# Down products of the last four inner blocks of a ReLU² MLP: float16 in three parts instead of fp32r in two

## Chip, cores and metric

The kernel runs on one core of a Trainium2 chip. The metric is the device time of one execution in microseconds (us). TensorE is called PE in the profile, its weight loads PEld, VectorE DVE, ScalarE ACT, GpSimd POOL, and SyncE, which issues most DMAs, SP.

## What is computed

Attention with a relative bias for 4 batches of 8 heads, 576 positions and head size 64; its result, as a matrix `x` of 2304 rows and 512 columns, goes through a two-layer MLP:

```
x = attn_out.transpose(0, 2, 1, 3).reshape(B * S, H * D)   # 2304 x 512
h = x @ w_in                                               # 512 x 2048
r = np.maximum(h, 0.0)
g = r * r
out = g @ w_out                                            # 2048 x 512
```

The inputs and the output are fp32. The products must come out at fp32's accuracy, so each factor is split into a high part and what is left over, and a product is a sum of three partial products.

## The kernel before

The first 320 us or so are attention, the rest is the MLP, and the change touches the MLP. The rows of `x` are taken in five blocks: n = 0 to 3 are 512 rows of each batch, and n = 4 (called `B` in the code) are the 4 times 64 rows left over. The 2048 inner columns are taken in eight inner blocks P = 0 to 7 (`NP` is 8). A pair (n, P) is an item; there are 40 of them, in the order that `runs` gives (L1171): items 0 to 11 are blocks 0, 1 and 2 with P = 0 to 3, items 12 to 17 block 3 with P = 0 to 5, items 18 to 31 blocks 0 to 3 with the rest of their P up to 7, and items 32 to 39 are block `B` with P = 0 to 7. So the inner blocks 4 to 7 are items 16 to 31, of full width (w = 256), and items 36 to 39, of half width (w = 128).

The loop at L1317 runs once for each item, and its iteration i works on item i and on the item before it:

- `products(i)` (L1198) makes the up products in a seven-product scheme (Strassen's): 42 float16 matmuls of w columns, 24 into the PSUM tile `ha` and 18 into `hb`.
- `parts_g(i-1)` (L1240) splits the squared activations `c` of the item before: ACT copies them to fp32r (`gh`), DVE subtracts (`gl`).
- `lead` and `high_out` or `sums_in`, `high_in`, `low_in` prepare one 128-row piece of a weight for later use: n = 4P+2 and 4P+3 are the pieces of `w_out` of inner block P. `lead_at` (L1179) says in which iteration. `high_out` (L727) makes an fp32r copy on ACT and the rest on POOL.
- `sums(i)` (L1214) puts the seven products together on ACT (one pass) and DVE (four) and scales them by `alpha`; `squares(i)` applies ReLU and the square, on ACT up to item 31, on DVE after that (`GA`, L1234).
- `down(i-1)` (L1287) makes the down products: 24 matmuls of 512 columns (12 for block `B`) into four (two) PSUM tiles `y`, a third with each of (gh, wh), (gh, wl), (gl, wh). At the end of a run `leave` (L1260) takes `y` out and stores it.

On PE the order is therefore `products(0)`, `products(1)`, `down(0)`, `products(2)`, `down(1)` and so on, written out by hand: under `manual_schedule` each engine works in program order, SP's queue too. Where iteration i-1 has looked for the largest entry of a block of x (`largest_at`: i-1 = 4, 8, 28), a one-column fp32 matmul with a matrix of ones (L1328) stands between `products(i)` and `down(i-1)`; it spreads a column's sum over all partitions, and five small DVE instructions after `sums(i)` (`scale_of`, L772, with `power_of`, L219) make a scale of it. Raw pieces of `w_out` come by DMA (`fetch_out`, L697); the last eight (18, 19, 22, 23, 26, 27, 30, 31) one per iteration from iteration 4 on (L1353).

Of the kernel before, what the change touches and what calls it, by code (L numbers as in the profile page):

```python
# [70 lines left out]
XC = 8  # L71
MAGIC = 8388608.0

HI_MIN, HI_MAX = (float(x) for x in np.array([0x38000000, 0x47EFFFFF], np.uint32).view(np.float32))
# [3 lines left out]
def attention_then_relu2_mlp(ctx: ExitStack, tc: tile.TileContext, q, k, v, cols, w_in, w_out, psi, xmat, dist, out):  # L78
# [101 lines left out]
    ins = [n for n in range(2 * NF) if n // 2 % 2 == 0]  # L180
    small = keep.tile([128, 72], F32, name="small")
    used = [0]

    def column(w=1):
        used[0] += w
        return small[:, used[0] - w:used[0]]

# [30 lines left out]

    def power_of(ps_col):  # L219
# [3 lines left out]
        DVE.tensor_scalar(out=ti, in0=ti, scalar1=0x7F800000, scalar2=None, op0=ALU.bitwise_and)  # L223
        DVE.tensor_scalar(out=si, in0=ti, scalar1=-1.0, scalar2=266 * 2.0 ** 23, op0=ALU.mult, op1=ALU.add)
        DVE.tensor_scalar(out=isig, in0=top, scalar1=2.0 ** -12, scalar2=None, op0=ALU.mult)
        return sig, isig
# [5 lines left out]

    def top_w():
        m = column()
        mi = m.bitcast(I32)
        largest(wcols, m)
        DVE.tensor_scalar(out=m, in0=m, scalar1=HI_MIN, scalar2=HI_MAX, op0=ALU.max, op1=ALU.min)
        t = column()
# [488 lines left out]
    def high_out(n):  # L727
        copy_out(n)
        rest_out(n)

# [34 lines left out]
    ORDER = (2, 3, 4, 5, 1, 6, 7)  # L765
    xs_t = {}

    def set_scale(n, cols, ps_col):
# [3 lines left out]
    def scale_of(n, ps_col):  # L772
        xsig[n], isig = power_of(ps_col)
        alpha_t[n] = column()
        DVE.tensor_tensor(out=alpha_t[n], in0=wscale[1], in1=isig, op=ALU.mult)
# [233 lines left out]
    def scan(k):  # L1009
        scan_w(k)  # L1010
        if k + len(raws) < NF:
            fetch_in(ins[k + len(raws)], raws[(k - SCANS) % len(raws)])
        if k == NF - 1:
            jobs.insert(len(norms), [now[0] + 1, [("DVE", 0.75, lambda: power_job(now[0] + 1, top_w(), scaled))]])
# [164 lines left out]
    lead_at = {1: (6, 7), 2: (10, 11), 3: (14,), 4: (15,)}  # L1179
    lead_at.update({5: (16,), 9: (17,), 12: (20,), 13: (21,), 14: (18, 19), 15: (22, 23)})  # L1180
    lead_at.update(zip(range(18, 26), ((n,) for n in range(24, 32))))
# [3 lines left out]
    largest_at = {4: 2, 8: 3, 28: B}  # L1185
    raw_outs = [18, 19, 22, 23, 26, 27, 30, 31]
    raw_ins = [n for n in ins if n not in early]
# [7 lines left out]
    c_t, g_t, y_t = {}, {}, {}  # L1195
    scales = []

# [16 lines left out]
    def sums(i, ha, hb):  # L1214
        n, P = items[i]
        w = width[n]
        alpha = alpha_t[n]
        if i % 2:
            c, s = (take(1, o, 1024).rearrange("p (m t) -> p m t", m=4)[:, :, :w] for o in (4480, 5504))
        elif i < NP // 2:  # L1220
            c, s = (tmp_p.tile([128, 4, 256], F32, name=x, tag=x) for x in "cs")
        else:
            c, s = (xT[1][:, :, 256 * x:256 * x + w] for x in range(2))
        ACT.activation(out=s, in_=ha[:, :, :w], func=AF.Identity, scale=alpha)
        stt = DVE.scalar_tensor_tensor
        stt(out=c[:, 2:4], in0=ha[:, 1:3, :w], scalar=alpha, in1=s[:, 0:4:3], op0=ALU.mult, op1=ALU.subtract)
        stt(out=c[:, 0:2], in0=ha[:, 2:4, :w], scalar=alpha, in1=s[:, 0:2], op0=ALU.mult, op1=ALU.add)  # L1227
        stt(out=c[:, 2:4], in0=hb[:, 0:1, :w].to_broadcast([128, 2, w]), scalar=alpha, in1=c[:, 2:4], op0=ALU.mult, op1=ALU.add)
        stt(out=c[:, 2:4], in0=hb[:, 1:3, :w], scalar=alpha, in1=c[:, 2:4], op0=ALU.mult, op1=ALU.add)
        c_t[i] = c  # L1230

    def squares(i):
# [4 lines left out]
        else:  # L1237
            DVE.scalar_tensor_tensor(out=c, in0=c, scalar=0.0, in1=c, op0=ALU.max, op1=ALU.mult)

    def parts_g(i):  # L1240
        c, w = c_t[i], width[items[i][0]]
        for f in range(2):
            gl = mlp.tile([128, 2, 256], F32R, name="gl", tag="gl", bufs=2)[:, :, :w]
            gh = mlp.tile([128, 2, 256], F32R, name="gh", tag="gh", bufs=2)[:, :, :w]
# [42 lines left out]
    def down(i):  # L1287
# [25 lines left out]
    with tc.manual_schedule():  # L1313
        for n in (6, 7, 10, 11, 14, 15):
            fetch_out(n)
        fetch_in(raw_ins.pop(0))
        for i in range(NI + 1):  # L1317
            if i == NP // 2:
# [106 lines left out]
```

## Time and profile before

| | us |
|---|---|
| median of 3 runs | 697.07 (697.04 to 697.47) |
| the profiled execution: its own time | 697.57 |
| its span, from the first to the last instruction | 695.8 |
| PE busy, share of the span | 97% |
| granted clock of PE, mean over the span | 0.997 |

The profiled execution's time is 1.8 us more than its span and 0.5 us above the median. The profile's views used below are the page (busy time by engine), the windows (busy time of each engine in a stretch), the chain of waits (the work that ended last, followed back), the timeline (instructions in order of time, merged where they repeat) and the groups of instructions by line and shape. A matmul's duration in these views is longer than the step from its start to the next one's start, since matmuls overlap in the pipeline; where the text needs the step it divides the time from one group's start to the next one's by the count.

### The profile page before, as it was taken

What the parts mean: (1) busy time and instruction counts of PE and PEld (TensorE: products, weight loads), DVE (VectorE), ACT (ScalarE), POOL (GpSimd) and SP (SyncE); (2) the same over time, 40 slices, a digit from 0 to 9 for tenths busy, and PEclk for the clock granted to TensorE, in tenths of its full rate; (3) what the DMA queues carried; (4) which work ended last, traced back from release to release, by engine and by line L of the source; (5) the groups of instructions that cost most, each with busy time, mean ns of one, the idle gap of its engine ahead of it and who ended that gap; (6) DMA issues with size and microseconds to landing.
All of it is one profiled execution on the core that took longest, in us unless ns stands there. A gap on an engine that the chain in (4) does not pass through costs nothing.

```text
span 695.8 us, 17950 instructions
## 1 busy us (share of the span) xinstructions
PE 676.8 (97%) x7238; PEld 561.5 (81%) x7238; DVE 549.9 (79%) x1165; ACT 473.2 (68%) x960; POOL 196.5 (28%) x313
## 2 busy tenths in 40 slices
PE   6899999999999999999999999999999999999997
PEld 5578888887877878778788888888888888888886
DVE  8999989877788898998888969777477775567664
ACT  5678888888777989997666756766466664447221
POOL 6465545442112343653223205112020112001000
PEclk9999999999999999999999999999999999999999
DMA  6740000017476134111901443050057222633101
GB/s 188 205 128 13 20 2 3 2 63 206 152 266 196 55 116 131 47 33 57 367 2 62 152 167 122 14 214 1 1 194 291 106 77 106 227 121 122 62 1 31
DMA packets 31682, 75.16 MB, mean 108 GB/s; under 512 B 5616, under 2 KB 13936, under 8 KB 30576
## 3 DMA queue, kind: packets, MB, share of 16 engines
q1 hardware_dynamic: 31440, 73.76, 31.1%
q8 instruction: 57, 0.93, 0.6%
q14 instruction: 25, 0.20, 0.1%
q10 hardware_dynamic: 160, 0.26, 0.1%
HBM read 55.66 MB, written 18.35 MB: 106 GB/s over the span
## 4 chain that ended last, share of the span: by engine, by line
PE 86%; DVE 8%; ACT 2%; issue 2%; POOL 1%; DMA 0%; ACTq 0%; POOLq 0%; DVEq 0%
PE y L1302 29%; PE ha L1210 13%; PE sp L425 11%; PE px L565 10%; PE hb L1210 10%; PE bb L383 5%; PE pp L529 3%; PE pp L534 3%; DVE t L438 2%; DVE mask L373 1%; PE pa L547 1%; ACT pt L1141 1%; DVE bt L391 1%; ACT p L445 1%; DVE xT L496 0%
## 5 line engine op out<-in xcount | busy, mean ns | idle before, releaser
L1210 PEld LDWEIGHTS <-area 128*128 128x128 f16 x1680 | 147.7, 98 | 25.3 <-issue 8.4
L1302 PE MATMUL y<-w,gh 128*128 128x512 f32 x576 | 149.0, 398 | 0.6 <-ACT gh L1246 0.6
L1302 PEld LDWEIGHTS y<-w,gh 128*128 128x128 f32 x576 | 105.1, 188 | 22.2 <-ACT gh L1246 1.3
L438 DVE CUSTOM_DVE_ANT_0 t<-sp,area 128x576 f32<-128x576 f32 x144 | 104.2, 753 | 21.2 <-PE sp L425 10.3
L445 ACT ACTIVATE p<-t,negm 128x576 f32<-128x576 f32 x144 | 112.9, 794 | 2.7 <-DVE negm L438 2.1
L425 PE MATMUL sp<-k,q 64*128 64x288 f32 (+1 forms) x640 | 99.4, 428 | 5.5 <-DVE negm L438 3.9
L565 PE MATMUL px<-pt,v 128*64 128x128 f32 (+1 forms) x1600 | 92.2, 266 | 0.0
L565 PEld LDWEIGHTS px<-pt,v 128*64 128x64 f32 x1600 | 79.2, 137 | 10.7 <-ACT pt L1141 6.0
L1210 PE MATMUL ha<-area 128*128 128x256 f16 (+1 forms) x816 | 85.1, 260 | 0.7 <-DVE c L1227 0.7
L399 POOL TENSOR_TENSOR area<-bt,bt 128x256 f32<-128x256 f32 x72 | 65.9, 922 | 64.1 <-DVE bt L391 63.9
L1302 PE MATMUL y<-w,gl 128*128 128x512 f32 x288 | 79.0, 390 | 0.0
L425 PEld LDWEIGHTS sp<-k,q 64*128 64x128 f32 (+1 forms) x640 | 53.3, 176 | 25.5 <-issue 6.0
L1210 PE MATMUL hb<-area 128*128 128x256 f16 (+1 forms) x612 | 64.7, 260 | 0.0
L1302 PEld LDWEIGHTS y<-w,gl 128*128 128x128 f32 x288 | 54.1, 188 | 12.2 <-DVE gl L1247 0.2
L373 DVE TENSOR_TENSOR mask<-sdist,theta 128x1024 f16<-128x1024 f16 x81 | 57.3, 711 | 1.0 <-PE bb L383 0.8
L869 ACT COPY pt<-pp 128x512 f32<-128x512 f32 (+1 forms) x76 | 37.4, 544 | 24.9 <-PE pp L534 24.7
L383 PEld LDWEIGHTS <-mask 128*128 128x128 f16 x1296 | 45.9, 99 | 9.5 <-DVE mask L373 6.4
L383 PE MATMUL bb<-wmov,mask 128*128 128x64 f16 x1296 | 47.5, 193 | 5.5 <-DVE mask L373 4.7
L1141 ACT COPY pt<-pp 128x512 f32<-128x512 f32 x76 | 41.4, 601 | 12.8 <-PE pp L529 12.3
L1247 DVE TENSOR_TENSOR gl<-area,gh 128x512 fp32r<-128x512 f32 (+1 forms) x40 | 25.3, 668 | 27.3 <-ACT gh L1246 25.5
L738 POOL TENSOR_TENSOR raw<-wa 128x256 f32<-128x256 f32 x16 | 12.2, 761 | 120.9 <-issue 66.1
L388 ACT ACTIVATE bt<-bb,small 128x256 f32<-128x256 f32 x81 | 39.1, 486 | 7.1 <-PE bb L383 5.2
(164 smaller groups left out, 1062.2 us busy)
## 6 DMA issues: line engine op xcount, KB each, us to landing
raw<-in_w_in SPq DMA_DIRECT2D x32, 512.0 KB, 4.4
r<-in_w_out SPq DMA_DIRECT2D x16, 512.0 KB, 5.4
xs<-area SPq DMA_DIRECT2D x4, 1792.0 KB, 11.1
py<-o SPq DMA_DIRECT2D x12, 512.0 KB, 4.1
o<-py SPq DMA_DIRECT2D x12, 512.0 KB, 4.1
v<-in_v SPq DMA_DIRECT2D x16, 320.0 KB, 4.0
q<-in_q SPq DMA_DIRECT2D x32, 128.0 KB, 3.0
out<-o SPq DMA_DIRECT2D x8, 512.0 KB, 2.9
```

What stands on the lines that cost most here:

```text
L373: DVE.tensor_tensor(out=out, in0=win, in1=th, op=ALU.is_ge)
L383: PE.matmul(bb[:, 64 * (7 - r):64 * (8 - r)], lhsT=m[:, r], rhs=wmov[:, n], start=(n == 0), stop=(n == 1))
L388: ACT.activation(out=sv, in_=bv[:, 1], func=AF.Identity, scale=bscale)
L399: POOL.tensor_tensor(out=dst, in0=tw, in1=sw, op=ALU.add)
L425: mm = PE.matmul(out_t[to, x, :HALF], lhsT=qt[rows, cols], rhs=kt[rows, k0:k0 + HALF], start=True, stop=True)
L438: DVE.tensor_tensor_reduce(out=t.rearrange("p (x n) -> p x n", x=2), in0=sp[:, :, :HALF], in1=bias.rearrange("p (x n) -> p x n", x=2), sca ...
L445: ACT.activation(out=p[:, S * n:S * n + S], in_=t, func=AF.Exp, bias=negm[:, n:n + 1], scale=-1.0, accum_out=sums[:, 2 * ic + n:2 * ic + n ...
L565: PE.matmul(px[64 * h:64 * h + 64, 128 * m:128 * m + w], lhsT=vt[:, c, h], rhs=src, start=(c == 0), stop=(c == 4))
L869: ACT.copy(dst, src)
L1141: ACT.copy(*c)
L1210: PE.matmul(h[:, s, :w], lhsT=a, rhs=x, start=(k == 0), stop=(k == 5))
L1302: PE.matmul(y_t[n][k], lhsT=(gl if m == 2 else gh)[:, slot, o:o + 128], rhs=wl if m == 1 else wh, start=((n, P) in firsts and f == 0 and m ...
```

## The change

All partial products of the inner blocks 4 to 7 become float16 by float16. A float16 has as many significant bits as are wanted of a high or low part but little range, so scales (powers of two) are worked out at run time. `w_out`'s late pieces are scaled and kept as three float16 parts: high, low, and high divided by 1024 (`fine`). The activations are kept as high divided by 1024 and the rest; the three partial products are (gh, high), (gh, low), (gl, fine). The units of `y` then differ from the result's by a power of two, which `leave` puts right. Inner blocks 0 to 3 keep fp32r. Cut to its core:

```diff
     def high_out(n):
-        copy_out(n)
-        rest_out(n)
+        if n < 2 * NP:
+            copy_out(n)
+            rest_out(n)
+            return
+        a = scratch[n].rearrange("p g n -> p (g n)")
+        t = home[n].tile([128, 3, 512], F16, name=f"w{n}", tag=f"w{n}", bufs=1)
+        hi, lo, fine = w_t[n] = [t[:, k] for k in range(3)]
+        POOL.tensor_scalar(out=a, in0=a, scalar1=oscale[0], scalar2=None, op0=ALU.mult)
+        ACT.copy(hi, a)
+        POOL.tensor_tensor(out=lo, in0=a, in1=hi, op=ALU.subtract)
+        ACT.activation(out=fine, in_=hi, func=AF.Identity, scale=1.0 / FINE)
...
-    lead_at.update({5: (16,), 9: (17,), 12: (20,), 13: (21,), 14: (18, 19), 15: (22, 23)})
+    lead_at.update({5: (16,), 9: (17,), 12: (20,), 13: (21,), 14: (18,), 15: (19,), 16: (22,), 17: (23,)})
...
-    raw_outs = [18, 19, 22, 23, 26, 27, 30, 31]
+    late_outs = [18, 19, 22, 23, 26, 27, 30, 31]
+    scan_at = {3: (18,), 4: (19, 22), 5: (23,), 6: (26,), 7: (27,), 8: (30,), 9: (31,)}
...
+    def scan_out(n):
+        k = late_outs.index(n)
+        largest(wraw_t[n][:, :, :, 1].bitcast(F32), ocols[:, k:k + 1])
...
+    def early_columns():
+        cols = column(NF + (B - 1) * HP)
+        values_of(wcols, cols[:, 0:NF])
+        squares_of(cols[:, 0:NF], wcols)
+        for n in range(B - 1):
+            squares_of(cols[:, NF + HP * n:NF + HP * n + HP], xcols[n])
+        return cols
+
+    def told_early(ps):
+        w2, top = wcols[:, 0:NF // 2], column()
+        DVE.tensor_reduce(out=w2, in_=ps[:, 0:NF].rearrange("p (n c) -> p n c", c=2), axis=AX.X, op=ALU.add)
+        DVE.tensor_reduce(out=top, in_=w2, axis=AX.X, op=ALU.max)
+        DVE.tensor_scalar(out=top, in0=top, scalar1=2.04, scalar2=None, op0=ALU.mult)
+        reach.append(top)
+        roots_of(0, B - 1, ps[:, NF:])
+
+    def roots_of(n, e, ps):
...
+        DVE.tensor_tensor(out=root[:, n:e], in0=alphas[:, n:e], in1=k, op=ALU.mult)
...
+    def told_x(n):
+        def then(ps):
+            scale_of(n, ps[:, 0:1])
+            if n >= B - 1:
+                roots_of(n, n + 1, ps[:, 1:])
...
+    def ask(i):
+        if i == 7:
+            return early_columns(), told_early
+        if i == 10:
+            return top_w(ocols), told_out
+        n = largest_at[i]
+        x_largest(n, xcols[n])
+        return scale_columns(n), told_x(n)
...
     def sums(i, ha, hb):
-        alpha = alpha_t[n]
+        alpha = alpha_t[n] if plain(n, P) else (root if P >= NP // 2 else lead_root)[:, n:n + 1]
...
     def parts_g(i):
...
+            if P >= NP // 2:
+                gl, gh = (mlp.tile([128, 4, 256], F16, name=x, tag=x, bufs=2)[:, 0:2, :w] for x in ("gl", "gh"))
+                g = c[:, 1 - f:4:2]
+                ACT.activation(out=gh, in_=g, func=AF.Identity, scale=1.0 / FINE)
+                DVE.scalar_tensor_tensor(out=gl, in0=gh, scalar=-FINE, in1=g, op0=ALU.mult, op1=ALU.add)
+                g_t[i, f] = (gh, gl)
+                continue
...
     def leave(n, P, k):
+        unit = 1.0 if plain(n, P) else beta[:, n:n + 1]
...
-            DVE.tensor_copy(out=o[:, 0], in_=y)
+            DVE.tensor_scalar(out=o[:, 0], in0=y, scalar1=unit, scalar2=None, op0=ALU.mult)
...
-            DVE.tensor_tensor(out=o[:, x], in0=o[:, x], in1=y, op=ALU.add)
+            DVE.scalar_tensor_tensor(out=o[:, x], in0=y, scalar=unit, in1=o[:, x], op0=ALU.mult, op1=ALU.add)
...
-            ACT.copy(o[:, x], y)
+            ACT.activation(out=o[:, x], in_=y, func=AF.Identity, scale=unit)
...
     def down(i):
-            wh, wl = w_t[4 * P + 2 + f]
+            wh, wl, *fine = w_t[4 * P + 2 + f]
...
-                y_t[n][k], lhsT=(gl if m == 2 else gh)[:, slot, o:o + 128], rhs=wl if m == 1 else wh,
+                y_t[n][k], lhsT=(gl if m == 2 else gh)[:, slot, o:o + 128], rhs=(wh, wl, *fine)[m] if fine else (wh, wl, wh)[m],
...
-            if i - 1 in largest_at:
-                PE.matmul(hb[:, 3, 0:1], lhsT=ones, rhs=scales[0], start=True, stop=True)
+            told = asked
+            if told:
+                ps = hb[:, 3, 0:told[0].shape[1]]
+                PE.matmul(ps, lhsT=ones, rhs=told[0], start=True, stop=True)
...
-            if i - 1 in largest_at:
-                scales.pop(0)
-                scale_of(largest_at[i - 1], hb[:, 3, 0:1])
+            if told:
+                told[1](ps)
...
-            if 4 <= i and raw_outs:
-                fetch_out(raw_outs.pop(0))
+            for m in late_outs[2 * i - 2:2 * i] if i else ():
+                fetch_out(m)
+            for m in scan_at.get(i, ()):
+                scan_out(m)
...
-            if i in largest_at:
-                scales.append(overall(x_largest(largest_at[i])))
+            asked = ask(i) if i in largest_at or i in (7, 10) else None
```

What is left out are small helpers on single columns (`values_of`, `squares_of`, `scale_columns`, `told_out`, `last_scales`, and the rest of `roots_of`), a few DVE instructions each; `told_out` follows the matmul of iteration 11.

## Rows read from the trace of the kernel before

**Rows 1.** The page: busy time, share of the span and instructions of each engine.

```profile
PE 676.8 (97%) x7238; PEld 561.5 (81%) x7238; DVE 549.9 (79%) x1165; ACT 473.2 (68%) x960; POOL 196.5 (28%) x313
```

**Rows 2.** Windows: length, busy us (instructions) of each engine, granted clock, DMA.

```profile
400.00:450.00 50.00, 50.00 (x330) 41.92 (x329) 38.96 (x60) 31.56 (x44) 10.86 (x11) 1.00 0.26 100
650.00:695.80 45.80, 41.36 (x399) 34.81 (x398) 26.89 (x57) 10.20 (x22) 0.00 (x0) 0.98 0.11 35
```

**Rows 3.** Chain of waits, iterations 8 to 10, then the end: start us, us, what.

```profile
406.13 5.49 PE y L1302 x24
411.62 2.64 PE ha L1210 x24
414.25 1.97 PE hb L1210 x18
...
416.33 5.70 PE y L1302 x24
...
426.63 5.48 PE y L1302 x24
...
685.50 2.82 PE y L1302 x12
688.33 3.06 PE y L1302 x12
```

**Rows 4.** Timeline of PE: up products of a full item, then of a half one.

```profile
411.46 2.79 PE L1210 MATMUL ha<-area 128*128 128x256 f16 x24
414.09 2.13 PE L1210 MATMUL hb<-area 128*128 128x256 f16 x18
...
677.80 1.51 PE L1210 MATMUL ha<-area 128*128 128x128 f16 x24
679.15 1.17 PE L1210 MATMUL hb<-area 128*128 128x128 f16 x18
```

**Rows 5.** Groups by line and shape: count | busy us, mean ns | idle before.

```profile
L1246 ACT CAST gh<-xT 128x512 fp32r<-128x512 f32 x28 | 16.1, 627 | 0.3
L803 ACT ACTIVATE area<-xT,small 128x512 f16<-128x512 f32 x16 | 10.7, 717 | 0.0
L810 DVE SCALAR_TENSOR_TENSOR area<-xT,small,area 128x512 f16<-128x512 f32 x16 | 11.3, 745 | 0.0
L725 POOL TENSOR_TENSOR w<-wa,w 128x512 fp32r<-128x512 f32 x16 | 20.6, 1290 | 81.1 <-ACT w L719 81.1
L752 POOL TENSOR_SCALAR area<-wa,small 128x256 f16<-128x256 f32 x8 | 7.9, 987 | 0.0
L204 DVE TENSOR_REDUCE small<-raw 128x1 f32<-128x512 f32 x16 | 10.2, 674 | 0.0
```

**Rows 6.** Timeline, iteration 9: DVE's small instructions and split, POOL's sums beside them.

```profile
419.08 2.56 POOL L797 TENSOR_TENSOR xT<-xT 128x512 f32<-128x512 f32 x2
...
420.24 0.14 DVE L225 TENSOR_SCALAR small<-small 128x1 f32<-128x1 f32 x1
420.42 1.23 DVE L775 TENSOR_TENSOR small<-small 128x1 f32<-128x1 f32 x1
...
423.88 1.28 DVE L1247 TENSOR_TENSOR gl<-area,gh 128x512 fp32r<-128x512 f32 x2
```

**Rows 7.** Timeline, iteration 19: last sum of DVE, next use of the PSUM tile.

```profile
520.44 0.75 DVE L1229 SCALAR_TENSOR_TENSOR area<-hb,small,area 128x512 f32<-128x512 f32 x1
...
522.86 1.38 PE L1210 MATMUL ha<-xT,area 128*128 128x256 f16 x11
```

**Rows 8.** The page, DMA issues: count, KB each, median us to landing.

```profile
r<-in_w_out SPq DMA_DIRECT2D x16, 512.0 KB, 5.4
```

**Rows 9.** Timeline, the last item's squares, split and first down products.

```profile
687.07 0.69 DVE L1238 SCALAR_TENSOR_TENSOR area<-area 128x512 f32<-128x512 f32 x1
...
687.87 0.71 ACT L1246 CAST gh<-area 128x256 fp32r<-128x256 f32 x2 [2.66 <-PE y L1302]
...
688.33 0.74 PE L1302 MATMUL y<-w,gh 128*128 128x512 f32 x2
```

More of the change, by code (lines that the diff above doesn't have):

```diff
@@ L72 @@
 MAGIC = 8388608.0
+FINE = 1024.0
 HI_MIN, HI_MAX = (float(x) for x in np.array([0x38000000, 0x47EFFFFF], np.uint32).view(np.float32))
@@ L180, in attention_then_relu2_mlp @@
     ins = [n for n in range(2 * NF) if n // 2 % 2 == 0]
-    small = keep.tile([128, 72], F32, name="small")
+    small = keep.tile([128, 76], F32, name="small")
     used = [0]
@@ L185, in column @@
         used[0] += w
-        return small[:, used[0] - w:used[0]]
+        return columns[0][:, used[0] - w:used[0]]
+    columns = [small]
     def lead_w(n, a, upto=7):
@@ L217, in power, with power_of @@
         return power_of(ps_col)
-    def power_of(ps_col):
+    def power_of(ps_col, mask=0x7F800000, most=12):
         top, sig, isig = (column() for _ in range(3))
@@ L222, in power_of @@
         ti, si = top.bitcast(I32), sig.bitcast(I32)
-        DVE.tensor_scalar(out=ti, in0=ti, scalar1=0x7F800000, scalar2=None, op0=ALU.bitwise_and)
-        DVE.tensor_scalar(out=si, in0=ti, scalar1=-1.0, scalar2=266 * 2.0 ** 23, op0=ALU.mult, op1=ALU.add)
-        DVE.tensor_scalar(out=isig, in0=top, scalar1=2.0 ** -12, scalar2=None, op0=ALU.mult)
+        DVE.tensor_scalar(out=ti, in0=ti, scalar1=mask, scalar2=None, op0=ALU.bitwise_and)
+        DVE.tensor_scalar(out=si, in0=ti, scalar1=-1.0, scalar2=(254.0 + most) * 2.0 ** 23, op0=ALU.mult, op1=ALU.add)
+        DVE.tensor_scalar(out=isig, in0=top, scalar1=2.0 ** -most, scalar2=None, op0=ALU.mult)
         return sig, isig
@@ L231, in scan_w, with top_w, values_of @@
         largest(wraw_t.pop(ins[k])[:, :, :, 1].bitcast(F32), wcols[:, k:k + 1])
-    def top_w():
+    def top_w(cols):
         m = column()
+        largest(cols, m)
+        return values_of(m)
+    def values_of(m, t=None):
         mi = m.bitcast(I32)
-        largest(wcols, m)
         DVE.tensor_scalar(out=m, in0=m, scalar1=HI_MIN, scalar2=HI_MAX, op0=ALU.max, op1=ALU.min)
-        t = column()
+        t = column() if t is None else t
         DVE.tensor_scalar(out=t.bitcast(I32), in0=mi, scalar1=3, scalar2=0x3FFFFFFF, op0=ALU.logical_shift_left, op1=ALU.bitwise_and)
@@ L766, in attention_then_relu2_mlp @@
     xs_t = {}
+    alphas = column(B + 1)
     def set_scale(n, cols, ps_col):
@@ L773, in scale_of @@
         xsig[n], isig = power_of(ps_col)
-        alpha_t[n] = column()
+        alpha_t[n] = alphas[:, n:n + 1]
         DVE.tensor_tensor(out=alpha_t[n], in0=wscale[1], in1=isig, op=ALU.mult)
@@ L1013, in scan @@
         if k == NF - 1:
-            jobs.insert(len(norms), [now[0] + 1, [("DVE", 0.75, lambda: power_job(now[0] + 1, top_w(), scaled))]])
+            jobs.insert(len(norms), [now[0] + 1, [("DVE", 0.75, lambda: power_job(now[0] + 1, top_w(wcols), scaled))]])
             for n in early[:4]:
@@ L1195, in attention_then_relu2_mlp, with squares_of @@
     c_t, g_t, y_t = {}, {}, {}
-    scales = []
+    columns[0], used[0] = xT[0][:, 0, 384:512], 0
+    ocols, beta, lead_root = column(len(late_outs)), column(NB), column(NB)
+    root, root_beta = column(NB), column(NB)
+    oscale, reach = [], []
+    xcols.extend(column(HP) for _ in range(AB, NB))
+    def scan_out(n):
+        k = late_outs.index(n)
+        largest(wraw_t[n][:, :, :, 1].bitcast(F32), ocols[:, k:k + 1])
+    def squares_of(dst, cols):
+        DVE.tensor_tensor(out=dst, in0=cols, in1=cols, op=ALU.mult)
@@ new lines, in scale_columns @@
+    def scale_columns(n):
+        if n < B - 1:
+            return overall(xcols[n])
+        cols = column(1 + HP)
+        squares_of(cols[:, 1:], xcols[n])
+        largest(xcols[n], cols[:, 0:1])
+        return cols
[5 more added lines that the diff above has]
+            squares_of(cols[:, NF + HP * n:NF + HP * n + HP], xcols[n])
+        return cols
@@ new lines, in told_early @@
+    def told_early(ps):
[6 more added lines that the diff above has]
+    def roots_of(n, e, ps):
+        ts = DVE.tensor_scalar
+        x2, k = column(e - n), column(e - n)
+        DVE.tensor_reduce(out=x2, in_=ps.rearrange("p (n c) -> p n c", c=HP), axis=AX.X, op=ALU.add if n < B else ALU.max)
+        ts(out=x2, in0=x2, scalar1=reach[0], scalar2=2.0 ** -100, op0=ALU.mult, op1=ALU.max)
+        if n == B:
+            ts(out=x2, in0=x2, scalar1=float(HP), scalar2=None, op0=ALU.mult)
+        xi, ki, ri = x2.bitcast(I32), k.bitcast(I32), root_beta[:, n:e].bitcast(I32)
+        ts(out=xi, in0=xi, scalar1=1, scalar2=0x7F800000, op0=ALU.logical_shift_right, op1=ALU.bitwise_and)
+        ts(out=ki, in0=xi, scalar1=-1.0, scalar2=202 * 2.0 ** 23, op0=ALU.mult, op1=ALU.add)
+        DVE.tensor_tensor(out=root[:, n:e], in0=alphas[:, n:e], in1=k, op=ALU.mult)
+        ts(out=ri, in0=xi, scalar1=1.0, scalar2=57 * 2.0 ** 23, op0=ALU.mult, op1=ALU.add)
@@ new lines, in told_x, with told_out @@
+    def told_x(n):
[3 more added lines that the diff above has]
+                roots_of(n, n + 1, ps[:, 1:])
+            if n == B:
+                last_scales(B, NB)
+        return then
+    def told_out(ps):
+        oscale.extend(power_of(ps, 0x7F000000, 11))
+        r = column()
+        DVE.tensor_scalar(out=r.bitcast(I32), in0=oscale[0].bitcast(I32), scalar1=0.5, scalar2=58.5 * 2.0 ** 23, op0=ALU.mult, op1=ALU.add)
+        oscale.append(r)
+        last_scales(0, B)
@@ new lines, in last_scales @@
+    def last_scales(a, b):
+        DVE.scalar_tensor_tensor(out=beta[:, a:b], in0=root_beta[:, a:b], scalar=oscale[1], in1=root_beta[:, a:b], op0=ALU.mult, op1=ALU.mult)
+        DVE.tensor_scalar(out=lead_root[:, a:b], in0=root[:, a:b], scalar1=oscale[2], scalar2=None, op0=ALU.mult)
+    def ask(i):
[6 more added lines that the diff above has]
+        return scale_columns(n), told_x(n)
@@ L1238, in squares, with plain @@
             DVE.scalar_tensor_tensor(out=c, in0=c, scalar=0.0, in1=c, op0=ALU.max, op1=ALU.mult)
+    def plain(n, P):
+        return n < B - 1 and P < NP // 2
     def parts_g(i):
-        c, w = c_t[i], width[items[i][0]]
+        (n, P), c = items[i], c_t[i]
+        w = width[n]
         for f in range(2):
+            if P >= NP // 2:
[5 more added lines that the diff above has]
+                continue
             gl = mlp.tile([128, 2, 256], F32R, name="gl", tag="gl", bufs=2)[:, :, :w]
@@ L1316, in attention_then_relu2_mlp @@
         fetch_in(raw_ins.pop(0))
+        asked = None
         for i in range(NI + 1):
```

## The prediction

> **What bounds the kernel now.** I read the page first. PE is busy in 97% of the span, DVE in 79%, ACT in 68% [rows 1]. A busy share alone proves nothing, so next come the windows: in the MLP's middle PE is busy in every one of 50.00 us, with DVE at 38.96, ACT at 31.56 and POOL at 10.86; only the last 45.8 us leave PE some idle time, 4.4 us [rows 2]. The granted clock there is 1.00 and 0.98, so PE sits at its upper level, 2.4 GHz, and has no clock to win. Third, the chain of waits, which shows what PE's time is made of. An item of full width is 5.49 us of down products, 2.64 of `ha` and 1.97 of `hb`, 10.10 in all, and then the next begins: the chain never leaves PE [rows 3]. So from about 335 us to 685 us the time is the sum of PE's steps, and a change counts by what it does to a step, as long as nothing else comes late.
>
> **The step of a down product.** 24 fp32r products of 512 columns take 5.49 us, 228.8 ns each [rows 3]. No product of 512 columns in float16 stands in the trace, but narrower ones do: 24 of 256 columns take 414.09 - 411.46 = 2.63 us, 109.6 ns each, and 24 of 128 columns 679.15 - 677.80 = 1.35 us, 56.3 ns [rows 4]. The second 128 columns cost 53.3 ns, which is one column per cycle at 2.4 GHz. Carried on, 512 columns take 109.6 + 2 x 53.3 = 216.2 ns. I take that value, since both rows are float16 with a weight load before each product, as the new ones are. The bounds: no better than two products of 256 less their fixed part, 213 ns (512 columns and nothing else), and no worse than the 228.8 of now. A gain of 0 to 15.8 ns, and 12.6 taken.
>
> **The sum, part by part.**
> - Items 16 to 31: 24 x 216.2 = 5.19 us instead of 5.49, 0.30 less for each of 16 items, **-4.8**. All of it lies on the chain.
> - Items 36 to 39, half width: 12 products are 2.59 us instead of 2.82 [rows 3], 0.23 less. For items 36 and 37 that is -0.46. Item 38's share only lengthens the wait that follows it: the last down products start when the last `gh` is there (DVE's squares from 687.07, `gh` from 687.87, products at 688.33 [rows 9]), and that chain hangs on `hb`, not on item 38. Item 39's own 12 products (3.06 us) save about 0.2, its wider `gh` gives about 0.1 back, so -0.1. Together **-0.6**.
> - Two more products with the ones matrix, in iterations 8 and 11. Of the one in iteration 9 the chain shows what it costs: 416.33 - 406.13 = 10.20 us before it and 426.63 - 416.33 = 10.30 with the block behind it, whose 24 products step more slowly (5.70 instead of 5.49): 0.3 us over two items of 10.10 [rows 3]. Here up to 28 columns instead of one, which can add a few tens of ns. Two of them: **+0.6**.
> - ACT: each `gh` becomes a scaled activation to float16, 717 ns where the copy takes 627 [rows 5], 0.2 us per item. Each of eight `w_out` pieces gets one more pass of about 0.7 us. DVE: `gl` becomes a scalar-tensor-tensor to float16, 745 ns [rows 5] instead of 640 [rows 6], 0.2 us per item. Cost nothing: in these stretches ACT and DVE are idle a third and a fifth of the time, and the tightest place I found after iteration 12 is iteration 19, where DVE ends its last sum at 521.19 and PE writes the tile again at 522.86 [rows 7], 1.67 us later. It shrinks by the 0.30 that PE gains.
> - POOL gets a scaling of 512 columns for each of the eight pieces. The nearest row is 987 ns for 256 columns [rows 5], so about 2.0; the lower end is the 1.29 that a subtraction of 512 takes [rows 5]. ACT's copy waits for it in the middle of an iteration, with the ReLU and the square queued behind it. DVE's `lead` ends before DVE's sums begin, so the copy comes at about the time the ReLU could start anyway; the delay is up to 1 us, and the first use of the squares lies several us later. Nothing on the chain.
> - DVE scans eight raw pieces, 0.67 us each [rows 5], one (once two) in each of iterations 3 to 9, and runs some 44 more single-column instructions at 0.15 us [rows 6], most in iterations 8 (9 of them), 9 and 11. The worst is iteration 9: 0.67 + 7 x 0.15 = 1.7 us more, and perhaps 1.2 on top (next paragraph). Behind these on DVE stand `gl` of item 9 and the sums of iteration 10. `gl` ends at 425.16 [rows 6] and is first needed 8 products into the block of 426.63 [rows 3], at 428.5. That leaves 3.3 us for 2.9: nothing, but little spare.
> - SP fetches the eight pieces in iterations 1 to 4 instead of 4 to 11. Pieces 18 and 19 are fetched two iterations, 20 us, before DVE's first scan asks for them, against 5.4 us to landing [rows 8]. The last two wait for the memory of `c` of item 2, and behind them SP holds one store of x that nobody waits for. Nothing.
> - `alpha` from another column, the scale in `leave`, and single leads in 14 to 17 instead of two pairs: the same passes over the same columns, off the chain. Nothing.
>
> Sum: -4.8 - 0.6 + 0.6 = -4.8 us on the profiled execution's 697.57, so 692.8; that execution lies 0.5 above the median, so **692.3 us** is my forecast for the median.
>
> **Where a rule meets the trace.** In iteration 9 a one-column multiply of DVE with two inputs takes 1.23 us, its neighbour 0.14; it ends with POOL's two sums, 419.08 to 421.64 [rows 6]. The Trainium skill, "SBUF — State Buffer", section "Who interferes with whom", says that a DVE instruction with two SBUF inputs cannot run beside a GpSimd one that reads SBUF, and that the later one waits for the whole of it. This speaks against a change that gives POOL more to read and DVE more two-input work; the row agrees. It is the 1.2 us above, and the third rival below.
>
> **Rivals.**
> 1. *The step does not depend on the number format.* A down product may step at 228.8 ns because of its 512 columns of fp32 sums, and not because of fp32r. For it: no float16 row of that width. Against it: 256 and 128 columns lie on a line of one column per cycle, and 228.8 ns lies 12.6 above that line. Then the gain is gone and the +0.6 stays: 697.7. The Trainium skill, "TensorE: Matmul & The Clock Gate", section "Back-to-back issue gap", gives a warm step as the columns over 2.4 plus 2.5 ns, with no word on the format; by that rule fp32r would step at about 216 ns too and nothing were to be won. The 228.8 ns disagrees with it for fp32r, while the float16 rows agree. Chance 0.07.
> 2. *Half of it.* The step comes out around 222 ns, or small waits of PE in iterations 3 to 11 take 2 to 3 us back (gh comes late, or a scan holds up the `lead` behind it). -2.4 instead of -4.8: 694.7. Chance 0.10.
> 3. *DVE comes late; slower than before.* Place: the eight iterations from 14 to 25 in which a `w_out` piece is made. POOL then reads SBUF for up to 2.0 + 1.3 us more or less in a row, and if `gl` or the two-input steps of `lead` fall into that, DVE loses up to 3.3 us and the sums behind them are late. It decides from 1.4 us on, the 1.67 of iteration 19 less 0.30. At 3.3 us PE would wait 1.9 us each time, 15 in all less the 4.8 gained: 707. Against it: POOL's new work begins when `lead` has ended, and DVE's next work is the sums, whose one operand is in PSUM. Chance 0.04.
>
> **Chances and range.** My forecast has 0.79. Its own spread: the step's bound of 213 ns (another -1.4), the ones matmuls (0 to +0.6) and small stalls. The range of 8 in 10 is 690.8 to 695.0: it takes in the forecast's spread and the half gain, and leaves out rivals 1 and 3 and the ends. About 0.2% (1.4 us) is what a measurement of this kernel can tell from no change. Faster by more than that: the forecast and most of rival 2, 0.88. Within it: rival 1 and a rest, 0.07. Slower: rival 3 and a rest, 0.05.
>
> **What would show it.** In the chain, the blocks of 24 down products from item 16 on should read 5.19 us instead of 5.49 and the item 9.8, with those before unchanged; those of 12 from item 36 on 2.59. DVE's windows of iterations 3 to 11 should be some 12 us fuller in sum, with PE still busy throughout. I am wrong if the float16 blocks stay near 5.49, or if PE shows waits for DVE or ACT in iterations 3 to 25 of more than a few tenths.

## The result and the profile after

The changed kernel takes 691.62 us (median of 4 runs, 691.18 to 692.27) and the kernel before 697.27 (median of 4, 697.04 to 698.51): a ratio of 0.9916, 95% interval 0.9899 to 0.9933, or 5.65 us less. The forecast was 692.3 us, with a range of 690.8 to 695.0. The profiled execution of the changed kernel took 692.27, the slowest of its four; its span is 690.5 us, against 695.8.

First the page's busy times and three windows of the changed kernel, beside [rows 1, 2] (columns as there).

```profile
PE 671.7 (97%) x7242; PEld 526.5 (76%) x7242; DVE 557.4 (81%) x1217; ACT 478.1 (69%) x968; POOL 209.2 (30%) x321
```

```profile
400.00:450.00 50.00, 50.00 (x332) 42.05 (x331) 43.55 (x97) 31.20 (x44) 11.01 (x11) 1.00 0.17 69
450.00:500.00 50.00, 50.00 (x330) 41.11 (x329) 33.06 (x53) 32.26 (x44) 12.79 (x11) 1.00 0.21 80
500.00:550.00 50.00, 50.00 (x337) 32.80 (x336) 35.97 (x60) 32.85 (x44) 10.94 (x13) 1.00 0.50 179
```

DVE, ACT and POOL all do more than before (+7.5, +4.9 and +12.7 us in the whole span), and PE is still busy for all of every 50 us, at the same granted clock. So the gain is no wait that went away; PE's own steps got shorter. The chain of waits of the changed kernel, beside [rows 3], shows which (start us, us, what):

```profile
406.37 0.14 PE hb L1438 x2
406.51 5.53 PE y L1409 x24
...
416.77 5.70 PE y L1409 x24
...
427.07 5.46 PE y L1409 x24
...
457.49 5.61 PE y L1409 x24
...
487.84 5.49 PE y L1409 x24
493.33 2.64 PE ha L1305 x24
495.96 1.97 PE hb L1305 x18
497.93 5.18 PE y L1409 x24
503.11 2.62 PE ha L1305 x24
...
507.69 5.18 PE y L1409 x24
...
675.48 2.59 PE y L1409 x12
...
683.26 2.81 PE y L1409 x12
```

At 493.33 the last fp32r block ends, after 5.49 us; the next is float16 and takes 5.18. The item goes from 10.09 to 9.76 us and stays there.

The whole difference, block by block: a step below is the time from the first recorded product of one block of down products to that of the next, so it holds one block and one item's up products. Step k starts with the block of item k-1: blocks 17 to 32 and 37 to 40 are the float16 ones.

| steps | before, us | after, us | sum of differences |
|---|---|---|---|
| 1 to 6, 12 to 15 | 10.08 to 10.43 | the same within 0.03 | 0.0 |
| 7 to 11 (the two new ones products) | 10.09, 10.31, 10.19, 10.08, 10.09 | 10.31, 10.27, 10.20, 10.28, 10.05 | +0.35 |
| 16 to 32 (float16, full width, from 17 on) | 10.05 to 10.09, but 10.31 in 28 and 7.88, 7.90 at the end | 10.17, then 9.76 or 9.77, but 9.91 in 28 and 7.52, 7.50 at the end | -5.1 |
| 33 to 36 | 5.18 to 5.22 | 5.15 to 5.21 | 0.0 |
| 37 to 39 (float16, half width) | 5.18, 5.18, 3.03 | 4.94, 4.93, 3.02 | -0.5 |
| from the start of the last block to the end | 7.42 | 7.23 | -0.2 |

(Steps 31 and 32 hold up products of half width. Step 16 is longer because the first float16 product is recorded 109 ns after the start of the product before it, an fp32r one 28 ns.) That is -5.5 us in the MLP. The two profiled executions also reach their first down block at different times, 334.70 and 334.98 us, though nothing ahead of it was changed; over all kernels profiled here that start lies between 333.96 and 335.30. So a single run's time carries up to 1.3 us that has nothing to do with the MLP, which is why the experiments are read by their steps first and by their times second.

### The profile page after: what moved, and what is told of

Read it like the earlier page. It is cut to its first block, busy times and chain, and to the rows that moved or that the text cites. A ratio compares the mean times of both kernels' runs of the same rounds, so it can differ in the third digit from the quotient of the medians.

```text
span 690.5 us, 18022 instructions
## 1 busy us (share of the span) xinstructions
PE 671.7 (97%) x7242; PEld 526.5 (76%) x7242; DVE 557.4 (81%) x1217; ACT 478.1 (69%) x968; POOL 209.2 (30%) x321
## 4 chain that ended last, share of the span: by engine, by line
PE 86%; DVE 8%; ACT 2%; issue 1%; POOL 1%; DMA 0%; ACTq 0%; POOLq 0%; DVEq 0%
PE y L1409 28%; PE ha L1305 13%; PE sp L431 11%; PE px L571 11%; PE hb L1305 10%; PE bb L389 5%; PE pp L535 3%; PE pp L540 3%; DVE t L444 2%; DVE mask L379 1%; PE pa L553 1%; ACT pt L1157 1%; ACT p L451 1%; DVE bt L397 1%; DVE xT L502 0%
## 5 line engine op out<-in xcount | busy, mean ns | idle before, releaser
L1409 PE MATMUL y<-w,gh 128*128 128x512 f32 (+1 forms) x576 | 143.5, 389 | 0.9 <-ACT gh L1352 0.6
L444 DVE CUSTOM_DVE_ANT_0 t<-sp,area 128x576 f32<-128x576 f32 x144 | 104.2, 754 | 21.8 <-PE sp L431 10.4
L1409 PE MATMUL y<-w,gl 128*128 128x512 f32 (+1 forms) x288 | 77.4, 385 | 0.0
L1409 PEld LDWEIGHTS y<-w,gh 128*128 128x128 f32 x288 | 52.5, 188 | 11.5 <-ACT gh L1352 0.9
L1409 PEld LDWEIGHTS <-gh 128*128 128x128 f16 x288 | 27.9, 98 | 30.2 <-ACT gh L1345 0.8
L535 PE MATMUL pp<-ident,p 128*128 128x128 f32 x304 | 39.9, 275 | 0.0
```

The source lines that it names most:

```text
L444: DVE.tensor_tensor_reduce(out=t.rearrange("p (x n) -> p x n", x=2), in0=sp[:, :, :HALF], in1=bias.rearrange("p (x n) -> p x n", x=2), sca ...
L535: PE.transpose(pp[:, 128 * c:128 * c + 128], p[:, k0:k0 + 128], ident)
L1409: PE.matmul(y_t[n][k], lhsT=(gl if m == 2 else gh)[:, slot, o:o + 128], rhs=(wh, wl, *fine)[m] if fine else (wh, wl, wh)[m], start=((n, P) ...
```

## The experiments

The edits of a_format_only, c_fp32r_halves and h_all_f16 are against the kernel before, of the others against the changed kernel. Where a kernel was run once, its time stands beside 696.91 us, a single run of the kernel before on the same chip.

### What the gain is made of

**The format alone** (a_format_only): float16 parts in inner blocks 4 to 7, with no scales, no scans, no ones products, and fetches and leads where they were.

```diff
     def high_out(n):
...
+        hi, lo, fine = w_t[n] = [t[:, k] for k in range(3)]
+        ACT.copy(hi, a)
+        POOL.tensor_tensor(out=lo, in0=a, in1=hi, op=ALU.subtract)
+        ACT.activation(out=fine, in_=hi, func=AF.Identity, scale=1.0 / 1024.0)
...
+            if items[i][1] >= 4:
...
+                ACT.activation(out=gh, in_=g, func=AF.Identity, scale=1.0 / 1024.0)
+                DVE.scalar_tensor_tensor(out=gl, in0=gh, scalar=-1024.0, in1=g, op0=ALU.mult, op1=ALU.add)
```

> The kernel before with float16 parts for the inner blocks 4 to 7 and nothing else: no scales, no scans, no new products with ones, fetches and leads where they were (the scaling is left out). If the gain is PE's step alone, blocks of 24 float16 products read 5.18 us, items 9.77, the first 16 items are as before, and the span is about 5.9 us under that of before (16 x 0.32, the half items' 0.5 and 0.3 where rows change over): ratio 0.9915. If the moved fetches and leads had a part in the gain, this gains clearly less than the changed kernel, under 5.3 us.

Measured: 690.92 us against 697.17, ratio 0.9908 (0.9895 to 0.9922), 6.25 us less. Steps 1 to 15 are those of before within 0.03, 17 to 30 are 9.76 (28: 9.91), 37 and 38 are 4.93 and 4.94: the changed kernel's gain without its costs. Nothing else in the change makes it faster.

**Everything but the format** (b_scales_only): the changed kernel with its scales, scans, fetches and ones products, but fp32r parts.

```diff
-FINE = 1024.0
+FINE = 1.0
...
-        t = home[n].tile([128, 3, 512], F16, name=f"w{n}", tag=f"w{n}", bufs=1)
+        t = home[n].tile([128, 2, 512], F32R, name=f"w{n}", tag=f"w{n}", bufs=1)
...
-            if P >= NP // 2:
-                gl, gh = (mlp.tile([128, 4, 256], F16, name=x, tag=x, bufs=2)[:, 0:2, :w] for x in ("gl", "gh"))
...
```

> The changed kernel with fp32r parts: all scans, scales, moved fetches and leads stay, FINE is 1, and the late products take two fp32r parts as before. If only PE counts, it is 0.4 us slower than before (two products with ones at 0.2 us each): ratio 1.0006, blocks of 24 at 5.49 us throughout. If DVE's 12 us of new work, or POOL's, is felt anywhere, it is slower by more than 1 us and PE shows waits for DVE or ACT in iterations 3 to 25.

Measured: 697.53 us (10 runs) against 697.17, ratio 1.0003 (0.9994 to 1.0012). Step 7 is 10.31 and step 10 is 10.28, as in the changed kernel; all others stay within 0.04 us of where they were before. The scales cost the two ones products, 0.4 us, and nothing else that shows. The two kernels together give -6.25 + 0.36 = -5.89 by medians, the change itself -5.65; from the first down block to the end of the span it is -5.9 + 0.5 = -5.4, the change itself -5.5.

**fp32r products cut in half** (c_fp32r_halves): each late down product as two of 256 columns, each of which starts and ends its own sum, so that nothing accumulates in these blocks.

```diff
+            parts = (slice(0, 256), slice(256, 512)) if P >= NP // 2 else (slice(0, 512),)
+            for z in parts:
+                PE.matmul(
+                    y_t[n][k][:, z], lhsT=(gl if m == 2 else gh)[:, slot, o:o + 128], rhs=(wl if m == 1 else wh)[:, z],
...
```

> The kernel before with each late down product cut into two of 256 columns, each with its own weight load, and without accumulation in those blocks (every half starts and ends its own sum). What makes an fp32r product step at 227 ns and more? If it is the 188 ns weight load plus a gap that no longer fits behind 213 ns of columns, a half steps at about 227 ns too: a full item gets 5.4 us longer, the kernel about 98 us. If it is a fixed extra of 11 to 13 ns per product, a half steps at 118 to 120 ns: 0.3 us per full item, 5 to 6 us in all. If it is in proportion to the columns, a half steps at 114 ns and nothing changes.

**float16 products cut in half** (d_f16_halves): the same edit on the changed kernel.

```diff
+            parts = (slice(0, 256), slice(256, 512)) if P >= NP // 2 else (slice(0, 512),)
+            for z in parts:
...
```

> The changed kernel with the same cut, again without accumulation in the late blocks. The float16 weight load takes 98 ns; up products of 256 columns step at 109 ns with it. By the same reasoning halves step at 109 ns, a full item gets 24 x 2.6 ns = 0.06 us longer, the kernel 1.1 us. If float16 halves step at 227 ns as well, the weight load is not what sets it.

Measured: 702.79 and 692.55 us, beside 696.91. The chain of c_fp32r_halves:

```profile
518.61 5.75 PE y L1304 x48
524.36 2.64 PE ha L1210 x24
527.00 1.97 PE hb L1210 x18
```

and that of d_f16_halves:

```profile
516.77 5.24 PE y L1411 x48
522.01 2.62 PE ha L1305 x24
```

The cut kernels do the same columns in twice as many products. For fp32r that costs 5.75 - 5.49 = 0.26 us a block, for float16 5.24 - 5.18 = 0.06. A half product steps at 5.75 / 48 = 120 ns in fp32r and 5.24 / 48 = 109 in float16; a whole one at 227 (below) and 5.18 / 24 = 216. So both formats take 107 ns for 256 more columns, one column per cycle at 2.4 GHz (the granted clock is 1.00 here), and fp32r has some 13 ns more than that on a product, at both widths, where float16 has 2.5: a difference of 11 ns. (227 is the steady part of an fp32r block; in most blocks of before the nine steps behind the first one take 224 to 236 ns.) The extra is not a wait for the whole of the longer weight load, which lasts far more than a step; one line of c_fp32r_halves, by its source line (duration min/median/max, ns):

```profile
L1304 PEld LDWEIGHTS y<-w,gh x864: 186/192/192, 335.3 to 696.0; 128*128 128x128 f32 x173
```

Loads of about 190 ns lie beside products that start every 120, so the loads overlap, and a load's length does not set the step. A half that steps at 227 ns, as a wait for its whole load would give, and an extra in proportion to the columns (some 114) both fall; it is the fixed extra. What it consists of is not shown: that a fixed part of the load lies in it is not ruled out.

**float16 everywhere** (h_all_f16): the edit of a_format_only for all eight inner blocks.

```diff
-            if items[i][1] >= 4:
+            if items[i][1] >= 0:
...
```

> The kernel before with float16 parts for all eight inner blocks and no scales at all (the scaling is left out): twice as many float16 products. If PE's step is all, items 3 to 15 also come to 9.77 and the half items 32 to 35 gain 0.24 each: 5 us under the format-only kernel, about 686 us. If the first four items are held by the split and by DVE rather than by PE (the first block waits for its own split with 0.05 to 0.5 us to spare), these gain nothing and the total is 4.0 to 4.5 us under the format-only kernel.

Measured: 685.87 us against 697.17, ratio 0.9839 (0.9826 to 0.9852), 5.05 us under a_format_only. Steps 3 and 5 to 30 are 9.76 or 9.77 (4, 8, 28: 9.91; 15: 9.88) and 33 to 38 are 4.93 or 4.94. Steps 1 and 2 went up, from 10.22 and 10.08 to 10.43 each: the chain of waits there, from 344 to 353 us, leaves PE for DVE's splits, leads and sums. The gain goes with the number of float16 products wherever DVE and ACT have the room, and the first two steps do not have it.

**One ones product in place of three** (g_one_question): the columns of both new ones products go into the old one of iteration 9.

```diff
-    scan_at = {3: (18,), 4: (19, 22), 5: (23,), 6: (26,), 7: (27,), 8: (30,), 9: (31,)}
+    scan_at = {3: (18,), 4: (19, 22), 5: (23,), 6: (26,), 7: (27,), 8: (30, 31)}
...
-        if i == 7:
-            return early_columns(), told_early
-        if i == 10:
-            return top_w(ocols), told_out
```

> The changed kernel with one product with ones at iteration 9 that carries everything, in place of three at iterations 8, 9 and 11; the scan of the last piece moves to iteration 8. If each of the two products saved costs 0.2 us and DVE's fuller iterations 8 and 9 stay covered, the down products from item 11 on start 0.4 us earlier: 691.2 where the changed kernel has 691.6. If DVE comes late in iteration 9 (some 1 us more there, 2.9 us of spare), the gain is gone or turned round.

Measured: 691.35 us (691.15 to 692.52) against 697.17, ratio 0.9919 (0.9906 to 0.9933). Steps 7 and 10 are back at 10.09 and 10.06; from the first down block to the last it takes 347.98 us instead of 348.28. The 0.30 is there in the steps, and too small to be told apart in the times (691.35 and 691.62).

### How much room the weight pieces have

**Two more POOL passes per piece** (e_pool_2more): a multiplication by one, twice, between POOL's scaling and ACT's copy.

```diff
         POOL.tensor_scalar(out=a, in0=a, scalar1=oscale[0], scalar2=None, op0=ALU.mult)
+        for _ in range(2):
+            POOL.tensor_scalar(out=a, in0=a, scalar1=1.0, scalar2=None, op0=ALU.mult)
         ACT.copy(hi, a)
```

> The changed kernel with two more POOL passes (by 1.0) ahead of ACT's copy of each late piece of w_out: 3.1 us more POOL work each time, with ACT's copy, the ReLU and the square queued behind it. If covered as I said, block starts do not move (within 0.2 us in all). If POOL's reads hold up DVE, PE waits in the eight iterations with a piece, several us in all.

**Five more** (f_pool_5more).

```diff
+        for _ in range(5):
+            POOL.tensor_scalar(out=a, in0=a, scalar1=1.0, scalar2=None, op0=ALU.mult)
```

> As the one before with five more passes, 7.8 us per piece. ACT's copy then comes about 7 us late, and the spare of the first gh (2.1 to 5.0 us in these iterations) is used up: PE waits for gh in most of the eight iterations, 1 to 4 us each, 10 to 30 us in all, and the wait is for ACT, not for DVE. If the spare was larger than I read it, nothing moves even now.

Measured: 709.38 and 749.76 us, beside 696.91: both expectations missed, by far. In e_pool_2more steps 15 to 18 are 11.37, 12.41, 12.40 and 11.35, and 20, 21, 24 and 25 are 11.82, 12.40, 12.10 and 12.40; the others keep to the changed kernel's but for 23 (10.23). Read together, its waits between 470 and 600 us (waiting line, what it waited for: us in total, times, longest) and one trip of its timeline, iteration 16, show why:

```profile
ACT w L744 <- POOL wa L743: 49.9, 8, 6.3
...
PE y L1411 <- ACT gh L1347: 10.8, 6, 2.5
```

```profile
488.43 0.67 ACT L198 ACTIVATE wa<-r 128x512 f32<-128x512 f32 x1
...
490.89 0.69 DVE L204 SCALAR_TENSOR_TENSOR wa<-r,wa 128x512 uint32<-128x512 uint32 x1
...
491.69 1.57 POOL L741 TENSOR_SCALAR wa<-wa,xT 128x512 f32<-128x512 f32 x1 [5.79 <-DVE wa L204]
...
493.34 3.06 POOL L743 TENSOR_SCALAR wa<-wa 128x512 f32<-128x512 f32 x2
496.44 0.62 ACT L744 CAST w<-wa 128x512 f16<-128x512 f32 x1 [6.33 <-POOL wa L743]
...
499.78 1.15 ACT L1347 ACTIVATE gh<-xT 128x512 f16<-128x512 f32 x2
...
500.84 0.66 ACT L198 ACTIVATE wa<-r 128x512 f32<-128x512 f32 x1
```

It is a ring through one engine that works in order. ACT's absolute value (L198) starts the lead; DVE's four steps, POOL's scaling, ACT's copy, the fine part, the ReLU, the square and `gh` follow; and only behind `gh` can ACT start the next iteration's absolute value. Here a trip takes 500.84 - 488.43 = 12.41 us, and once such trips, longer than PE's item, have used up what `gh` is ahead, PE waits for it. The same line of the changed kernel:

```profile
483.10 0.69 ACT L198 ACTIVATE wa<-r 128x512 f32<-128x512 f32 x1
...
486.39 1.56 POOL L741 TENSOR_SCALAR wa<-wa,xT 128x512 f32<-128x512 f32 x1 [5.95 <-DVE wa L204]
487.99 0.62 ACT L742 CAST w<-wa 128x512 f16<-128x512 f32 x1 [0.96 <-POOL wa L741]
...
489.53 1.08 PE L1409 MATMUL y<-w,gl 128*128 128x512 f32 x4
489.95 1.06 ACT L1330 ACTIVATE xT<-xT 128x1024 f32<-128x1024 f32 x1 [0.68 <-DVE xT L1324]
490.44 1.98 PE L1409 MATMUL y<-w,gh 128*128 128x512 f32 x8
...
492.13 1.15 ACT L1345 ACTIVATE gh<-xT 128x512 f16<-128x512 f32 x2
492.26 1.07 PE L1409 MATMUL y<-w,gl 128*128 128x512 f32 x4
...
493.19 0.66 ACT L198 ACTIVATE wa<-r 128x512 f32<-128x512 f32 x1
```

(PE's fp32r products stand between: 489.53 to 492.26 is 12 products of 227 ns.) The trip is 10.09 us here, PE's own pace. Without the two passes e_pool_2more's would be 12.41 - (496.44 - 493.34) = 9.3 us, so beside a float16 item of 9.76 about 0.45 us is spare. (Where the changed kernel's own trip has nothing else to wait for, in iteration 21 from 524.83 to 534.08, it takes 9.25.) Five passes of 1.55 on 9.3 are 17.05, and steps 15 to 17 of f_pool_5more are 17.10, 17.12 and 17.11.

**One more pass** (k_pool_1more).

```diff
+        for _ in range(1):
+            POOL.tensor_scalar(out=a, in0=a, scalar1=1.0, scalar2=None, op0=ALU.mult)
```

> The changed kernel with one more POOL pass per late piece (1.53 us). By the ring, 12.40 less 1.53 is 10.87 us round, 1.1 more than PE's 9.77; the spare in front of the first gh (4.2 us) is used up by 1.53 once and 1.1 for each further iteration in a row, so PE waits at most about 1 us, near the end of the row of four pieces (iterations 14 to 17), and nowhere else: 692 to 693 us. If every pass costs its own length wherever it stands, it is half of what two passes cost: 8 to 9 us, 700 us.

Measured: 698.11 us beside 696.91, 5.8 us of span more than the changed kernel. Steps 15 to 17 do not move (10.09, 10.17, 9.76), then 18 is 11.21, 20 and 21 are 10.25 and 10.83, 23 to 25 are 10.58, 10.53 and 10.83. The length of a trip was right (two of them in the timeline, 528.42 to 539.25 to 550.08, 10.83 each), the total was not. The first three trips, 0.7 to 1.1 us longer than their items, use up a head start: the first half of `gh` ends 2.66, 1.92, 1.26, 0.19 and 0.05 us ahead of blocks 15 to 19 (in the changed kernel 4.23, 4.93, 5.00, 4.68 and 2.09), and only then, in step 18, does PE wait, by 1.4 us. So far that is much as expected. But the items between pairs were taken to give the delay back, and they do not: in iteration 22, with a piece of `w_in`, the absolute value at 550.08 leads to a `gh` that ends at 559.35, 9.3 us as well, and in iteration 23 the absolute value waits another 1.70 us for its piece's DMA (1.32 in the changed kernel). So the ring has as little to spare there as in the pairs.

**The same two passes, with the copies behind the squares** (j_pool_2more_behind): e_pool_2more, with `high_out` of the late pieces after `squares(i)` in ACT's order.

```diff
+            behind = one is not None and not is_in(one) and one >= 2 * NP
-            if one is not None:
+            if one is not None and not behind:
                 (sums_in if is_in(one) else high_out)(one)
...
                 squares(i)
+            if behind:
+                high_out(one)
```

> The kernel with two more POOL passes, and the late pieces' high_out moved behind the squares in program order; same work. The theory: what lengthens the items to 12.40 us is a ring through consecutive iterations, not POOL's port: ACT's abs of the next piece stands behind gh, which stands behind the square, the ReLU and the copy of this piece, which waits for POOL, which waits for DVE's lead, which waits for the abs. With ReLU and square taken out of the ring (2.1 us) it is 10.3 to 10.4 us round: items with a piece in each iteration read 10.3 to 10.4 instead of 12.40, single ones 9.76, and the kernel is about 695 us. If it is POOL's reading that holds up DVE, moving ACT's copy changes little: 12 us per item and some 709 us again.

Measured: 692.33 us beside 696.91, span 690.5, with POOL doing all that it did in e_pool_2more. All steps are the changed kernel's but step 25 (10.21). Its timeline, iteration 16:

```profile
489.40 3.07 POOL L743 TENSOR_SCALAR wa<-wa 128x512 f32<-128x512 f32 x2
...
490.45 1.06 ACT L1332 ACTIVATE xT<-xT 128x1024 f32<-128x1024 f32 x1 [3.82 <-DVE xT L1326]
...
492.51 0.61 ACT L744 CAST w<-wa 128x512 f16<-128x512 f32 x1
...
493.69 1.13 ACT L1347 ACTIVATE gh<-xT 128x512 f16<-128x512 f32 x2
```

POOL's passes now lie beside the squares instead of ahead of them, and 17 us are gone. So POOL's work cost e_pool_2more its time through the order of ACT, and not by keeping DVE from memory while it reads: DVE's sum beside the passes takes 0.75 us in both kernels.

The expected 10.3 to 10.4 us were right for the trip and wrong for the items. The trip takes 10.22 us (absolute values at 484.50 and 494.73), yet the items stay at 9.76, because the head start of `gh` covers the difference. It falls from 3.26 us ahead of block 15 to 0.07 and 0.06 ahead of blocks 25 and 26, where the 0.45 us of step 25 show. The passes are covered because the row of pieces ends there, not because the trip fits.

**Leads in pairs again** (i_lead_pairs): the changed kernel with the old entry for the leads.

```diff
-    lead_at.update({5: (16,), 9: (17,), 12: (20,), 13: (21,), 14: (18,), 15: (19,), 16: (22,), 17: (23,)})
+    lead_at.update({5: (16,), 9: (17,), 12: (20,), 13: (21,), 14: (18, 19), 15: (22, 23)})
```

> The changed kernel with the leads of pieces 18, 19, 22 and 23 in pairs in iterations 14 and 15, as in the kernel before. In a pair the second high_out comes behind the squares. If the moved leads matter, it is because two pieces in one iteration lengthen the ring: abs, lead and split twice, some 3 us more, in two consecutive iterations. The first gh has 4 to 5 us of spare there, so I expect no more than 2 us, at items 15 and 16, and the rest unchanged. If the leads were moved for no reason that shows, block starts differ by less than 0.2 us.

Measured: 696.81 us beside 696.91. Steps 15 and 16 are 12.60 and 11.79 instead of 10.09 and 10.17, 4.1 us together where at most 2 were expected, and all others are as in the changed kernel. Its timeline, iteration 15:

```profile
482.68 0.62 ACT L742 CAST w<-wa 128x512 f16<-128x512 f32 x1 [3.16 <-POOL wa L741]
...
488.67 0.62 ACT L742 CAST w<-wa 128x512 f16<-128x512 f32 x1 [2.11 <-POOL wa L741]
...
489.86 1.12 ACT L1352 CAST gh<-area 128x512 fp32r<-128x512 f32 x2
490.51 3.68 PE L1409 MATMUL y<-w,gh 128*128 128x512 f32 x8 [2.27 <-ACT gh L1352]
```

Two pieces in one iteration send ACT round by POOL twice ahead of the next `gh`, and PE waits 2.27 us for it. In a_format_only the pairs stand at the same place and steps 15 and 16 do not move (10.09, 10.17): with no scaling on POOL, ACT has nothing to wait for.

## Why the prediction was right, point by point

The forecast lies 0.7 us above the result. The mechanism is the one that was named, and three terms of the sum came out a little small, all to the same side.

- **The step of a float16 product**: 216.2 ns carried on from narrower ones [rows 4], 216 measured. Rival 1 and the 222 ns of rival 2 fall. Here the Trainium skill, "TensorE: Matmul & The Clock Gate", section "Back-to-back issue gap" (columns over 2.4 plus 2.5 ns), agrees with float16 at both widths, 216 and 109 ns, and not with fp32r, 227 and 120; the measurement decides. The section gives that formula for a product by itself, and about 131 ns at 512 columns for a stream of weight loads and products; the prediction left this out, and the 216 ns of this stream do not agree with it.
- **Items 16 to 31**: -4.8 forecast, -5.1 measured, the largest part of what the sum was short by. A float16 block also spares its neighbour: the `ha` block behind it takes 2.62 us instead of 2.64. Counted as 24 steps and nothing around them, the term came out 0.02 us an item too small.
- **Half items and the end**: -0.6 forecast, -0.5 in steps 37 to 39 and -0.2 behind them.
- **The ones products**: +0.6 forecast, +0.35 measured. The 0.3 for each was a misreading of [rows 3]: the slow block of 5.70 us was put down to the ones product ahead of it, but it is a block of inner block 0, and such blocks are slow without one too (block 13 above, 5.61), while block 8 of the changed kernel, behind its 0.14 us of ones product, takes 5.53. What is left for a ones product is some 0.2 us; the allowance for 28 columns in place of one was not needed (169 to 272 ns for the matmuls of all shapes from 1 to 28 columns).
- **DVE**: some 12 us more were forecast for its windows of iterations 3 to 11, and from 350 to 450 us they hold 5.7 more (43.76 and 38.96 before, 44.87 and 43.55 after). The scans are there, eight of 675 ns, and the small instructions too. But DVE got some back. In iteration 9 the 256-column instruction that took 1.58 us beside POOL's sums now starts when they have ended and takes 0.47. The two `gl` ahead of block 7 took 3.13 us before and take 1.29 now. Together that is 2.9 of the missing 6.3; the rest is not accounted for.

```profile
419.50 2.60 POOL L813 TENSOR_TENSOR xT<-xT 128x512 f32<-128x512 f32 x2
422.06 1.29 POOL L813 TENSOR_TENSOR area<-xT 128x512 f32<-128x512 f32 x1
```

```profile
421.57 1.58 DVE L756 SCALAR_TENSOR_TENSOR area<-wa,small,area 128x256 f16<-128x256 f32 x1
```

```profile
420.86 1.27 DVE L791 TENSOR_TENSOR small<-small,xT 128x1 f32<-128x1 f32 x1
...
423.35 0.47 DVE L771 SCALAR_TENSOR_TENSOR area<-wa,small,area 128x256 f16<-128x256 f32 x1
...
425.13 1.28 DVE L1353 TENSOR_TENSOR gl<-area,gh 128x512 fp32r<-128x512 f32 x2
```

  The first and third group are rows of the changed kernel's timeline, iteration 9 (POOL, then DVE), and answer to [rows 6]; the row between them is of the kernel before. `gl` ends at 426.4, well ahead of its use, so the cost of nothing was right there.
- **ACT and the splits**: `gh` takes 622 to 625 ns instead of the 717 taken, `gl` 686 to 701 instead of 745, the scaling 1566 instead of 2000. All three had been taken higher than they came out.

```profile
L1345 ACT ACTIVATE gh<-xT 128x512 f16<-128x512 f32 x16 | 9.2, 625 | 0.2
L1346 DVE SCALAR_TENSOR_TENSOR gl<-gh,area 128x512 f16<-128x512 f16 x16 | 10.6, 701 | 17.0 <-ACT gh L1345 17.0
L741 POOL TENSOR_SCALAR wa<-wa,xT 128x512 f32<-128x512 f32 x8 | 12.5, 1566 | 52.4 <-DVE wa L204 52.4
```

- **POOL's scaling and the single leads, "nothing"**: the outcome was right and the reasons were not. The scaling was said to delay the copy by up to 1 us, with several us to spare before the squares are used; but the delay hands itself on to the next iteration through ACT, and of the 9.76 us of an item 9.3 are taken. Had the scaling lasted the 2.0 us that were assumed, the ring would have been at 9.7. And the leads' move, costed as the same passes at another time, is worth 4.1 us: in i_lead_pairs the MLP takes 359.7 us from its first down block to the end (before 361.05, changed kernel 355.5), so without that move 1.3 us of the gain would have been left.
- **Rival 3** did not come, and it had the place wrong. It put the danger on DVE, through POOL's reading; j_pool_2more_behind shows that POOL can read for 3 us longer at no cost to DVE's sums, and e, f, k and i that the narrow place is ACT's order. That e_pool_2more's 709 us lie near the rival's 707 is a coincidence of two different mechanisms.

## What to carry to other kernels

On a chain that never leaves one engine, a change is worth the steps that it shortens: measure the step in a block that already runs that way, at two widths, and carry the line on. Room for work beside such a chain is not the idle time of an engine in a window, but, when an in-order engine takes part in every iteration, the time of one whole trip from its instruction in one iteration to the same in the next, held against the iteration's length. A trip that is longer stays hidden until the head start that the chain's input has gathered is used up, so a short row of such iterations can cost nothing and a longer one not. An instruction that waits for another engine belongs behind, in program order, whatever the chain needs from its own engine.

## What was not expected of the hardware

- An fp32r product has some 13 ns more on top of its columns, at 512 (227 ns) and at 256 (120) alike, where a float16 one has 2.5; a wait for the whole of the longer load (190 ns against 98) is not the reason.
- The fp32r blocks of inner block 0 are slower than the others, with a ones product ahead of them (416.77: 5.70 us) or without (457.49: 5.61, against 5.46 to 5.49); their products step at 229 to 240 ns to the end. In float16 the difference is gone: in h_all_f16 steps 5, 9 and 13 are 9.76 us, in the kernel before 10.19, 10.19 and 10.21. Why is not shown.
- A ones product of 1 to 28 fp32 columns costs PE some 0.2 us in all, whatever its width.
